# Retention and a mixture of experts on one core: the query's decay applied on the way out of PSUM, another order of the second product's units, closing sums and low parts spread over more steps

## The chip, the cores and the metric

The kernel runs on one core of a Trainium2 chip. The metric is the device time of one execution in microseconds (us); less is better. Of the kernel before three runs are shown, and one execution was taken by the hardware profiler. PE is TensorE, DVE is VectorE, ACT is ScalarE, POOL is GpSimd, SP is SyncE, whose queue issues nearly all DMAs.

## The reference

```python
# retention: per head a decaying state, 4 batches, 8 heads, 768 steps, 64 wide
for t in range(S):
    state = gamma * state + einsum('bhd,bhe->bhde', k[:, :, t], v[:, :, t])
    y[:, :, t] = scale * einsum('bhd,bhde->bhe', q[:, :, t], state)
# x = y as [3072 tokens, 512]; then 4 experts, 512 -> 1024 -> 512
p = probs / (probs.sum(-1) + 1e-9)
out = sum over e of  p[:, e] * (maximum(x @ w1[e], 0) @ w2[e])
```

All inputs and outputs are fp32.

## The kernel before, in words

**Retention.** Each batch of 768 tokens is cut into 6 chunks of 128. For a chunk, `scores` multiplies k and q of all heads (16 small matmuls, L140) into two PSUM banks, DVE multiplies them with a mask (L143), `state` adds the chunk's k times v to the running state (L155, L157, L159), POOL scales that by the decay of a chunk (`decay`, L165), and `values` forms the output of the chunk in two halves: q times the state before (L182) and masked scores times v (L188), in two PSUM banks, each of which ACT then copies into `xraw` (L197). Two factors are put on by POOL beforehand: `scale_q` (L124) multiplies the chunk's q in place by a table `qs` (scale times a power of the head's decay), `scale_v` (L128) multiplies v by a table `ks`.

**Experts.** A fast scheme with seven products in place of eight is used for both products of each expert, so that x and the hidden activations appear as seven combinations each, numbered 1 to 7. Each operand is split into a high part (ACT, fp32r) and a low part (the rest), and each product is three matmuls (high high, high low, low high) of 128x384. A **round** n (64 of them, 16 for each batch) makes 256 hidden columns: 7 **steps**, one `p1` each (6 matmuls, L502), in the order `SEQ`. Seven combinations of x serve a batch: in the last round of a batch each step issues `x_hi` of the next batch (ACT, L236), and one step later `x_lo` (L240; POOL for steps 1 and 3, DVE for the five others), through the list `late`.

**Second product.** In batch 0 (rounds 0 to 15) `p2` (L537) computes it plainly while weights are prepared and stored to DRAM. From batch 1 on, hidden columns are made by `gated` (DVE L454, POOL subtractions L456), split by `op_hi` (ACT L442) and `op_lo` (L447: on POOL for combinations 5, 7, 6 and 4, named in `LO_POOL`, else on DVE), and consumed by `unit(q, k)`: for a pair q of rounds 14 units, 6 matmuls each (L563), in the order `UNITS`, a combination i and a half d (0, 1) per unit. Pair q's units are issued in the steps of the next two rounds, one behind each `p1`, so that a step of 6 + 6 matmuls takes about 2.08 us. Units use two PSUM banks in turn; `add` on DVE (L420) adds each unit's result to one of 14 running sums. So a unit's matmuls wait until DVE has added the unit two before.

**Closing.** With the last pair of a batch, `finish` (L573) combines the seven sums of each half into four outputs by additions in SBUF (L576), on POOL and DVE by the table in the code, and stores them (L582, SP queue). For batches 1 and 2 that happens in the first two rounds of the next batch, while x's low parts are also due; for batch 3 after the last round, in a tail of 14 units that have no `p1` beside them.

**Order.** All is issued in one hand-written order. `soon` holds pairs (steps to wait, action), and `pass_step` runs what is due at the start of a step. `att_steps` is a generator that issues the attention of the next batch in pieces between the steps of the present one; the main loop takes one piece every few steps. At the start of a chunk it issues `decay`, `scale_q` and `scale_v`; the first `scores` of a batch comes right behind them. Before round 0 the six chunks of batch 0 run by themselves, with the first weights and x's parts prepared on DVE, ACT and POOL (the start-up, up to about 46 us).

Of the kernel before, what the change touches and what calls it, by code (L numbers as in the profile page):

```python
# [14 lines left out]
C = 128  # L15
# [24 lines left out]

UNITS = tuple((i, d) for i in (1, 3, 5, 7, 6, 2, 4) for d in range(2))
A2_AT = {1: 0, 2: 2, 4: 3, 6: 4, 7: 5, 3: 6, 5: 7}
LO_POOL = (5, 7, 6, 4)


@with_exitstack
def retention_moe(ctx: ExitStack, tc: tile.TileContext, qk, kv, w1, w2, probs, probt, cmask, cqs, cks, cys, out, out_t):
# [29 lines left out]
    ps_a = ep(tc.tile_pool(name="ps_a", bufs=2, space=PS))  # L79

    mask = const.tile([128, C], F32, name="mask")
    qs = const.tile([128, NPAIR, C], F32, name="qs")
    ks = const.tile([128, H], F32, name="ks")
    ys = const.tile([128, NPAIR], F32, name="ys")

# [36 lines left out]
    def scale_q(ci, eng=nc.gpsimd):
        q = raw_qk[ci][:, 0]
        eng.tensor_tensor(out=q, in0=q, in1=qs, op=ALU.mult)  # L124

    def scale_v(ci):
        v = raw_kv[ci][:, 1]
# [42 lines left out]
    def values(ci, half):  # L170

        b, c = divmod(ci, NCHB)
        v = raw_kv[ci]
        sp = sprime[ci]
        if half == 0:
            pvs[ci] = [att_bank("ps_v"), att_bank("ps_v")]
        ps = pvs[ci]
        quad = [(r, k) for r in range(2) for k in range(2)]
        if c > 0:
            for r, k in quad:  # L180
                rows, p = slice(64 * r, 64 * r + 64), 2 * half + k
# [12 lines left out]
        if c == 0:  # L194
            xraw[b] = xr_p.tile([128, NPAIR, S], F32, tag="xr", name="xr")
        for r in range(2):
            nc.scalar.activation(out=xraw[b][:, 2 * r:2 * r + 2, c * C:(c + 1) * C], in_=ps[r][:, 0:2, :], func=ACTF.Copy)  # L197


    xcomb = {}  # L200
# [371 lines left out]

    def finish(b, i, d):  # L573
        p = {j: psum[b, j, d] for j in range(1, 8)}
        e1, e2 = (nc.gpsimd, nc.vector) if b < B - 1 else (nc.vector, nc.gpsimd)
        sums = lambda e, o, x: e.tensor_tensor(out=p[o], in0=p[o], in1=p[x], op=ALU.add)  # L576

        def store(j, f, h):

            rows = out_t[256 * f + 128 * d:256 * f + 128 * d + 128]  # L580
            to = rows[:, (b - 1) * S + HB * h:(b - 1) * S + HB * h + HB]
            soon.append((2, lambda: nc.sync.dma_start(out=to, in_=p[j])))  # L582

        if i == 1:
            sums(e1, 2, 1)
        elif i == 5:
            sums(e1, 3, 5)
        elif i == 6:
            sums(e2, 6, 1)
            sums(e2, 7, 6)  # L590
            sums(e2, 4, 7)
            sums(e1, 3, 6)
            store(3, 0, 1)
            sums(e1, 5, 7)
            store(5, 1, 1)
        elif i == 2:
            store(2, 0, 0)
        elif i == 4:
            store(4, 1, 0)


    def att_steps(b):
        ci0 = b * NCHB
        load_qk(ci0 + 1)
        for ci in range(ci0, ci0 + NCHB):
            old = ci > ci0
            decay(ci)
# [24 lines left out]
    with tc.manual_schedule():  # L632
# [1 line left out]
        nc.vector.memset(warm, 0.0)  # L634
        load_qk(0)
        load_kv(0, eng=nc.scalar)
        nc.sync.dma_start(out=qs, in_=cqs)
        nc.scalar.dma_start(out=ks, in_=cks)
        nc.scalar.dma_start(out=mask, in_=cmask)
        load_qk(1, v_p, "w2h")  # L640
        load_kv(1)
        nc.scalar.dma_start(out=ys, in_=cys)
# [57 lines left out]
        values(ci, 1)  # L700

        steps = iter(())
        late = []
        for n in range(NRND * B):
            g, r = divmod(n, NRND)
            if r == 0 and g + 1 < B:
# [9 lines left out]
            for k, i in enumerate(SEQ if n else FIRST):  # L716
# [52 lines left out]
def _layout(q, k, v, moe_domain_probs, moe_w1, moe_w2):  # L769
# [26 lines left out]
    cqs = scale * gp[:, :, None] ** (t + 1 - C)[None, None, :]  # L796
# [22 lines left out]
```

## Time and profile before

| | us |
|---|---|
| runs, median (lowest to highest) | 1109.12 (1108.71 to 1111.15), 3 runs |
| the profiled execution | 1108.82 |
| its span | 1106.7 |
| PE busy in the span | 1069.9 (97%) |
| DVE, ACT, POOL busy | 716.0 (65%), 391.9 (35%), 707.5 (64%) |

The span runs from the first to the last instruction of the profiled execution; 2.1 us of that execution lie outside it. Busy times are averages over very unlike stretches: the start-up, batch 0, three batches with units, and the tail. The page's slices show PE at 9 tenths or more in most of the 40 slices, and less in the first, in two in the middle and in the last. The granted clock is 2.4 GHz (1.0 in the profile's rows) or half of it (0.5); a row's figure is a mean over its stretch.

### The profile page before, as it was taken

The numbers are of one execution on the slowest core, as the hardware profiler recorded it, in microseconds if no ns is written. First come the engines' busy times: TensorE is split into PE (matmuls) and PEld (weight loads), VectorE is DVE, ScalarE is ACT, GpSimd is POOL, SyncE is SP. The second block draws the span as 40 slices with busy tenths as digits, with TensorE's granted clock in tenths as the row PEclk, the third lists the DMA queues.
The fourth block names the chain that finished last, engine by engine and source line by source line (L and its number), as shares of the span: only waits on it lengthen the run. The fifth ranks groups of instructions, "written<-read, shape, count | busy, mean of one in ns | idle before, by whom it ended". The sixth has DMA issues, their size and how long they took to land.

```text
span 1106.7 us, 18610 instructions
## 1 busy us (share of the span) xinstructions
PE 1069.9 (97%) x6696; PEld 996.6 (90%) x6696; DVE 716.0 (65%) x1174; ACT 391.9 (35%) x785; POOL 707.5 (64%) x661
## 2 busy tenths in 40 slices
PE   7889999999999999999998999999999899999996
PEld 5678888888889999999998999999999899999995
DVE  5767566666676466666685455676668746667665
ACT  2434444444434422322341433223234343333230
POOL 5668676766637754754677666557468855555555
PEclk9899999999999999999998999999999999999998
DMA  8499989898899777877886887887788888887874
GB/s 319 143 307 306 305 304 354 290 321 296 266 340 321 248 259 261 263 241 259 255 252 212 283 272 218 277 269 221 236 254 252 275 265 255 264 261 251 266 221 152
DMA packets 154603, 293.70 MB, mean 265 GB/s; under 512 B 12688, under 2 KB 77328, under 8 KB 154512
## 3 DMA queue, kind: packets, MB, share of 16 engines
q1 hardware_dynamic: 153936, 291.92, 80.9%
q8 instruction: 53, 0.87, 0.3%
q10 hardware_dynamic: 576, 0.60, 0.2%
q14 instruction: 38, 0.31, 0.1%
HBM read 223.22 MB, written 69.26 MB: 264 GB/s over the span
## 4 chain that ended last, share of the span: by engine, by line
PE 87%; DVE 5%; POOL 4%; issue 3%; DMA 1%; ACT 0%; SPq 0%; POOLq 0%; DVEq 0%; ACTq 0%
PE ps_u L563 30%; PE ps_x L502 23%; PE ps_z L502 11%; PE ps_o L537 10%; PE ps_y L502 6%; PE ps_v L188 2%; PE ps_s L140 2%; DVE xl L240 1%; PE ps_v L182 1%; DVE sum L576 1%; PE ps_y L155 1%; POOL sum L576 1%; POOL qk L124 1%; POOL ol L447 1%; DVE sum L420 1%
## 5 line engine op out<-in xcount | busy, mean ns | idle before, releaser
L563 PE MATMUL ps_u<-oh,v 128*128 128x384 f32 x1344 | 397.9, 338 | 13.2 <-DVE sum L420 13.1
L456 POOL TENSOR_TENSOR b<-b 128x384 f32<-128x384 f32 x192 | 206.7, 1077 | 146.4 <-DVE b L454 118.2
L447 POOL TENSOR_TENSOR ol<-b,oh 128x384 fp32r<-128x384 f32 x192 | 208.2, 1096 | 101.6 <-ACT oh L442 51.9
L563 PEld LDWEIGHTS ps_u<-oh,v 128*128 128x128 f32 x1344 | 249.7, 189 | 16.6 <-DVE sum L420 16.6
L420 DVE TENSOR_TENSOR sum<-ps_u,sum 128x384 f32<-128x384 f32 x294 | 162.0, 552 | 146.4 <-PE ps_u L563 146.3
L442 ACT ACTIVATE oh<-b 128x384 fp32r<-128x384 f32 x336 | 163.0, 520 | 196.6 <-POOL b L456 106.9
L502 PE MATMUL ps_x<-xh,v 128*128 128x384 f32 x768 | 229.5, 340 | 0.3 <-ACT u L414 0.3
L563 PE MATMUL ps_u<-ol,v 128*128 128x384 f32 x672 | 226.1, 337 | 0.0
L414 ACT ACTIVATE u<-ps_x 128x384 f32<-128x384 f32 x128 | 62.7, 490 | 248.3 <-PE ps_x L502 248.1
L502 PEld LDWEIGHTS ps_x<-xh,v 128*128 128x128 f32 x768 | 142.4, 189 | 4.2 <-issue 2.3
L447 DVE TENSOR_TENSOR ol<-b,oh 128x384 fp32r<-128x384 f32 x144 | 127.3, 884 | 12.9 <-ACT oh L442 12.9
L502 PE MATMUL ps_x<-xl,v 128*128 128x384 f32 x384 | 129.1, 336 | 0.0
L563 PEld LDWEIGHTS ps_u<-ol,v 128*128 128x128 f32 x672 | 127.4, 190 | 0.0
L502 PE MATMUL ps_z<-xh,v 128*128 128x384 f32 x384 | 114.7, 339 | 0.4 <-DVE xl L240 0.3
L545 DVE SCALAR_TENSOR_TENSOR acc<-ps_o,pm,acc 128x512 f32<-128x512 f32 x90 | 67.0, 745 | 59.7 <-PE ps_o L537 59.7
L537 PE MATMUL ps_o<-w2h,hl 128*128 128x512 f32 x192 | 75.8, 395 | 0.0
L537 PE MATMUL ps_o<-w2l,hh 128*128 128x512 f32 x192 | 75.8, 395 | 0.0
L537 PE MATMUL ps_o<-w2h,hh 128*128 128x512 f32 x192 | 75.2, 392 | 0.0
L502 PEld LDWEIGHTS ps_z<-xh,v 128*128 128x128 f32 x384 | 70.8, 188 | 2.8 <-issue 1.0
L502 PEld LDWEIGHTS ps_x<-xl,v 128*128 128x128 f32 x384 | 72.5, 189 | 0.1
L502 PE MATMUL ps_z<-xl,v 128*128 128x384 f32 x192 | 64.2, 334 | 0.0
L420 DVE TENSOR_TENSOR ps_y<-ps_y,u 128x384 f32<-128x384 f32 x64 | 36.1, 565 | 40.6 <-PE ps_y L502 40.6
(108 smaller groups left out, 1680.7 us busy)
## 6 DMA issues: line engine op xcount, KB each, us to landing
v<-k SPq DMA_DIRECT2D x336, 256.0 KB, 3.7
v<-k SPq DMA_DIRECT2D x168, 512.0 KB, 4.4
k<-w1h SPq DMA_DIRECT2D x16, 896.0 KB, 6.3
k<-w1l SPq DMA_DIRECT2D x16, 896.0 KB, 8.5
qk<-in_qk SPq DMA_DIRECT2D x24, 512.0 KB, 5.9
kv<-in_kv SPq DMA_DIRECT2D x23, 512.0 KB, 6.4
w1r<-in_w SPq DMA_DIRECT2D x16, 512.0 KB, 7.9
w2r<-in_w SPq DMA_DIRECT2D x16, 512.0 KB, 4.2
```

The source lines that it names most:

```text
L140: nc.tensor.matmul(ps[r][:, p, :], lhsT=a[rows, 1, p, :], rhs=a[rows, 0, p, :], start=True, stop=True)
L188: nc.tensor.matmul(ps[r][64 * k:64 * k + 64, half, :], lhsT=v[:, 1, h, :], rhs=sp[:, h, :], start=(c == 0), stop=True, skip_group_check=True,)
L414: nc.scalar.activation(out=t, in_=ps, func=ACTF.Copy)
L420: nc.vector.tensor_tensor(out=o, in0=ps, in1=u, op=ALU.add)
L442: nc.scalar.activation(out=hi, in_=t, func=ACTF.Copy)
L447: eng.tensor_tensor(out=lo, in0=t, in1=hi.bitcast(F32), op=ALU.subtract)
L456: sub = lambda o, a, b: nc.gpsimd.tensor_tensor(out=o, in0=a, in1=b, op=ALU.subtract)
L502: nc.tensor.matmul(ps, lhsT=lhsT[:, cs], rhs=rhs[:, kt, :], start=(fresh and m == 0), stop=(m == 5), skip_group_check=True,)
L537: nc.tensor.matmul(ps, lhsT=a[:, ts], rhs=b[:, fs, :], start=(m == 0), stop=(m == 5))
L545: nc.vector.scalar_tensor_tensor(out=acc[nt], in0=ps, scalar=sc, in1=acc[nt], op0=ALU.mult, op1=ALU.add)
L563: nc.tensor.matmul(ps, lhsT=w[:, r, l, ds], rhs=o, start=(m == 0), stop=(m == 5))
L576: sums = lambda e, o, x: e.tensor_tensor(out=p[o], in0=p[o], in1=p[x], op=ALU.add)
```

## The change

1. `scale_q` goes, with its 24 POOL instructions. The table `qs` is laid out by bank and loaded on ACT's queue behind the mask, not second on SP's. Where `values` left PSUM by two ACT copies for each chunk (48 in all), DVE now multiplies each bank by `qs[:, r]` into `xraw`.
2. `UNITS` has the combinations in the order 1, 3, 6, 7, 5, 4, 2 in place of 1, 3, 5, 7, 6, 2, 4.
3. `finish`: per half, POOL does 2+=1, 6+=1, 7+=6, 4+=7, 7+=5 and DVE 3+=6, 3+=5, in all batches, each through `soon` with a wait of 0 to 2 steps. Before, POOL did 2+=1, 3+=5, 3+=6, 5+=7 and DVE 6+=1, 7+=6, 4+=7 at once (engines the other way round in batch 3). 4+=7 is now added to sum 4 ahead of the last unit of that sum. The four stores follow with waits of 0 to 2.
4. `x_lo` is issued up to 5 steps after its `x_hi` (`XLATE`) for batches 2 and 3, through `soon`.

The core of the diff:

```diff
-UNITS = tuple((i, d) for i in (1, 3, 5, 7, 6, 2, 4) for d in range(2))
+UNITS = tuple((i, d) for i in (1, 3, 6, 7, 5, 4, 2) for d in range(2))
+XLATE = (1, 2, 2, 3, 4, 4, 5)
-    qs = const.tile([128, NPAIR, C], F32, name="qs")
+    qs = const.tile([128, 2, 2, C], F32, name="qs")
-    def scale_q(ci, eng=nc.gpsimd):
-        q = raw_qk[ci][:, 0]
-        eng.tensor_tensor(out=q, in0=q, in1=qs, op=ALU.mult)
         for r in range(2):
-            nc.scalar.activation(out=xraw[b][:, 2 * r:2 * r + 2, c * C:(c + 1) * C], in_=ps[r][:, 0:2, :], func=ACTF.Copy)
+            o = xraw[b][:, 2 * r:2 * r + 2, c * C:(c + 1) * C]
+            nc.vector.tensor_tensor(out=o, in0=ps[r][:, 0:2, :], in1=qs[:, r], op=ALU.mult)
...
-        e1, e2 = (nc.gpsimd, nc.vector) if b < B - 1 else (nc.vector, nc.gpsimd)
-        sums = lambda e, o, x: e.tensor_tensor(out=p[o], in0=p[o], in1=p[x], op=ALU.add)
+        e1, e2 = nc.gpsimd, nc.vector
+        def sums(wait, e, o, x):
+            soon.append((wait, lambda: e.tensor_tensor(out=p[o], in0=p[o], in1=p[x], op=ALU.add)))
-        def store(j, f, h):
+        def store(wait, j, f, h):
...
         if i == 1:
-            sums(e1, 2, 1)
-        elif i == 5:
-            sums(e1, 3, 5)
-        elif i == 6:
-            sums(e2, 6, 1)
-            sums(e2, 7, 6)
-            sums(e2, 4, 7)
-            sums(e1, 3, 6)
-            store(3, 0, 1)
-            sums(e1, 5, 7)
-            store(5, 1, 1)
+            sums(0, e1, 2, 1)
+        elif i == 6:
+            sums(0, e1, 6, 1)
+            sums(2, e2, 3, 6)
+        elif i == 7:
+            sums(0, e1, 7, 6)
+            sums(1, e1, 4, 7)
+        elif i == 5:
+            sums(0, e1, 7, 5)
+            sums(0, e2, 3, 5)
+            store(2, 7, 1, 1)
+            store(2, 3, 0, 1)
+        elif i == 4:
+            store(1, 4, 1, 0)
         elif i == 2:
-            store(2, 0, 0)
-        elif i == 4:
-            store(4, 1, 0)
+            store(0, 2, 0, 0)
...
                     x_hi(g + 1, i)
-                    late.append(lambda b=g + 1, i=i, e=nc.gpsimd if k in XPOOL else nc.vector: x_lo(b, i, eng=e))
+                    e = nc.gpsimd if k in XPOOL else nc.vector
+                    soon.append((XLATE[k] - 1 if g else 0, lambda b=g + 1, i=i, e=e: x_lo(b, i, eng=e)))
```

What the change moves, at three places. Numbers behind a name tell one buffer from another; a line number above 124 is up to two less in the changed kernel, and L576 became L578.

POOL, first steps of batch 2 (round 32). The names: `sum` are the running sums, `ol` low parts of combinations, `b` their subtractions, `qk` and `kv` the first chunk of batch 3. Before:

```order
L456 TENSOR_TENSOR b_6206<-b_6206,b_6174 128x384
L576 TENSOR_TENSOR sum_3875<-sum_3875,sum_3582 128x384
L447 TENSOR_TENSOR ol_6304<-b_6174,oh_6303 128x384
L576 TENSOR_TENSOR sum_3902<-sum_3902,sum_3609 128x384
L447 TENSOR_TENSOR ol_6331<-b_6234,oh_6330 128x384
L447 TENSOR_TENSOR ol_6334<-b_6206,oh_6333 128x384
L456 TENSOR_TENSOR b_6259<-b_6259,b_6206 128x384
L124 TENSOR_TENSOR qk_5323<-qk_5323,qs_112 128x512
L128 TENSOR_TENSOR kv_5325<-kv_5325,ks_113 128x512
```

and now:

```order
L456 TENSOR_TENSOR b_6188<-b_6188,b_6156 128x384
L447 TENSOR_TENSOR ol_6283<-b_6156,oh_6282 128x384
L578 TENSOR_TENSOR sum_3915<-sum_3915,sum_3568 128x384
L447 TENSOR_TENSOR ol_6310<-b_6215,oh_6309 128x384
L447 TENSOR_TENSOR ol_6313<-b_6188,oh_6312 128x384
L578 TENSOR_TENSOR sum_3947<-sum_3947,sum_3595 128x384
L456 TENSOR_TENSOR b_6240<-b_6240,b_6188 128x384
L127 TENSOR_TENSOR kv_5307<-kv_5307,ks_113 128x512
```

The multiplication of `qk` is gone, and each sum stands one low part later.

DVE, round 33, from the units 6 and 7 on. `sum<-ps_u` is a unit's addition, `sum<-sum` a closing one. Before:

```order
L420 TENSOR_TENSOR sum_3813<-ps_u_6524,sum_3813 128x384
L576 TENSOR_TENSOR sum_3813<-sum_3813,sum_3582 128x384
L576 TENSOR_TENSOR sum_3761<-sum_3761,sum_3813 128x384
L576 TENSOR_TENSOR sum_3929<-sum_3929,sum_3761 128x384
L447 TENSOR_TENSOR ol_6511<-b_6460,oh_6510 128x384
L420 TENSOR_TENSOR sum_3851<-ps_u_6556,sum_3851 128x384
L576 TENSOR_TENSOR sum_3851<-sum_3851,sum_3609 128x384
L576 TENSOR_TENSOR sum_3784<-sum_3784,sum_3851 128x384
L576 TENSOR_TENSOR sum_3962<-sum_3962,sum_3784 128x384
L420 TENSOR_TENSOR ps_y_6572<-ps_y_6572,u_6484 128x384
```

and now:

```order
L420 TENSOR_TENSOR sum_3747<-ps_u_6445,sum_3747 128x384
L578 TENSOR_TENSOR sum_3636<-sum_3636,sum_3687 128x384
L420 TENSOR_TENSOR sum_3770<-ps_u_6469,sum_3770 128x384
L156 COPY yst0_115<-ps_y_6477 128x256
L578 TENSOR_TENSOR sum_3658<-sum_3658,sum_3725 128x384
L420 TENSOR_TENSOR sum_3799<-ps_u_6510,sum_3799 128x384
L447 TENSOR_TENSOR ol_6495<-b_6441,oh_6494 128x384
L578 TENSOR_TENSOR sum_3636<-sum_3636,sum_3799 128x384
L420 TENSOR_TENSOR sum_3837<-ps_u_6540,sum_3837 128x384
L578 TENSOR_TENSOR sum_3658<-sum_3658,sum_3837 128x384
L420 TENSOR_TENSOR ps_y_6553<-ps_y_6553,u_6467 128x384
```

Two runs of three closing sums have become four single ones with a unit's addition between them; of these, the first two read sums 6 (3687, 3725), to which POOL has added 1.

POOL, the tail, to the end of the program. Before:

```order
L447 TENSOR_TENSOR ol_12238<-b_12169,oh_12237 128x384
L576 TENSOR_TENSOR sum_9989<-sum_9989,sum_9780 128x384
L576 TENSOR_TENSOR sum_9937<-sum_9937,sum_9989 128x384
L576 TENSOR_TENSOR sum_10095<-sum_10095,sum_9937 128x384
L576 TENSOR_TENSOR sum_10017<-sum_10017,sum_9808 128x384
L576 TENSOR_TENSOR sum_9960<-sum_9960,sum_10017 128x384
L576 TENSOR_TENSOR sum_10115<-sum_10115,sum_9960 128x384
```

and now, from the low parts of 5, 7 and 6 on:

```order
L447 TENSOR_TENSOR ol_12169<-b_12078,oh_12168 128x384
L578 TENSOR_TENSOR sum_10071<-sum_10071,sum_9758 128x384
L447 TENSOR_TENSOR ol_12185<-b_12126,oh_12184 128x384
L447 TENSOR_TENSOR ol_12188<-b_12104,oh_12187 128x384
L578 TENSOR_TENSOR sum_10091<-sum_10091,sum_9785 128x384
L456 TENSOR_TENSOR b_12145<-b_12145,b_12104 128x384
L447 TENSOR_TENSOR ol_12214<-b_12145,oh_12213 128x384
L578 TENSOR_TENSOR sum_9866<-sum_9866,sum_9758 128x384
...
L578 TENSOR_TENSOR sum_9936<-sum_9936,sum_9993 128x384
```

POOL's six sums at the end have become ten, of which two stand between and behind the low parts; rows left out are six more sums.

## Rows read from the trace of the kernel before

**Rows 1.** Window: PE, PEld, DVE, ACT, POOL busy; granted clock, DMA share, GB/s.

```profile
345.00:570.00 225.00, 224.97 (x1481) 215.18 (x1480) 140.40 (x246) 78.59 (x172) 142.60 (x134) 1.00 0.80 259
```

**Rows 2.** Waits of PE over the whole span: us in total, times, longest.

```profile
PE ps_u L563 <- DVE sum L420: 13.1, 9, 2.6
```

**Rows 3.** Timeline of PE: start, duration, instruction, [idle before, releaser]; scores.

```profile
61.62 1.99 PE L140 MATMUL ps_s<-qk 64*128 64x128 f32 x16 [2.41 <-POOL qk L124]
584.66 2.08 PE L140 MATMUL ps_s<-qk 64*128 64x128 f32 x16 [4.09 <-POOL qk L124]
```

**Rows 4.** Timeline of PE: units at the two batch ends.

```profile
575.08 0.45 PE L563 MATMUL ps_u<-oh,v 128*128 128x384 f32 x1 [1.21 <-DVE sum L420]
609.93 0.44 PE L563 MATMUL ps_u<-oh,v 128*128 128x384 f32 x1 [1.79 <-DVE sum L420]
845.40 0.44 PE L563 MATMUL ps_u<-oh,v 128*128 128x384 f32 x1 [1.22 <-DVE sum L420]
867.10 0.45 PE L563 MATMUL ps_u<-oh,v 128*128 128x384 f32 x1 [0.60 <-DVE sum L420]
872.07 0.45 PE L563 MATMUL ps_u<-oh,v 128*128 128x384 f32 x1 [2.59 <-DVE sum L420]
```

**Rows 5.** Windows around the four drops of the granted clock (PEclk, third from the end).

```profile
61.00:66.00 5.00, 4.38 (x25) 4.07 (x26) 2.81 (x4) 1.44 (x2) 3.00 (x4) 0.66 1.07 380
583.00:592.00 9.00, 7.34 (x36) 7.12 (x37) 3.44 (x7) 1.46 (x3) 3.06 (x4) 0.62 0.43 147
611.00:615.00 4.00, 4.00 (x16) 4.00 (x15) 3.90 (x9) 0.57 (x2) 4.00 (x4) 0.57 0.85 257
1095.00:1104.00 9.00, 5.81 (x18) 4.99 (x18) 3.55 (x7) 0.00 (x0) 4.45 (x4) 0.62 0.37 132
```

**Rows 6.** Groups by line: busy, mean ns of one | idle before, releasers.

```profile
L124 POOL TENSOR_TENSOR qk<-qk,qs 128x512 f32<-128x512 f32 x24 | 32.3, 1345 | 6.6 <-DMA qs<-in_cqs 6.6
L197 ACT ACTIVATE xr<-ps_v 128x256 f32<-128x256 f32 x48 | 15.8, 380 | 43.7 <-PE ps_v L188 43.7
L159 DVE TENSOR_TENSOR yst<-ps_y,yst 128x256 f32<-128x256 f32 x16 | 6.8, 422 | 12.1 <-PE ps_y L155 11.9
L576 DVE TENSOR_TENSOR sum<-sum 128x384 f32<-128x384 f32 x20 | 18.0, 899 | 4.8 <-POOL sum L576 4.3
```

**Rows 7.** Timeline of DVE at the end of batch 1.

```profile
604.92 3.35 DVE L576 TENSOR_TENSOR sum<-sum 128x384 f32<-128x384 f32 x3
```

**Rows 8.** Timeline of POOL: the multiplication of q that PE waits for at 584.66.

```profile
583.34 1.27 POOL L124 TENSOR_TENSOR qk<-qk,qs 128x512 f32<-128x512 f32 x1
```

**Rows 9.** Timeline of POOL and then of PE in a steady pair of rounds of batch 3.

```profile
908.80 2.31 POOL L447 TENSOR_TENSOR ol<-b,oh 128x384 fp32r<-128x384 f32 x2 [1.06 <-PE ps_u L563]
914.50 0.33 PE L563 MATMUL ps_u<-ol,v 128*128 128x384 f32 x1
```

**Rows 10.** Timeline of the tail: a unit on PE, POOL, DVE's last addition.

```profile
1078.12 0.33 PE L563 MATMUL ps_u<-oh,v 128*128 128x384 f32 x1
1081.37 3.90 POOL L447 TENSOR_TENSOR ol<-b,oh 128x384 fp32r<-128x384 f32 x3
1091.87 7.74 POOL L576 TENSOR_TENSOR sum<-sum 128x384 f32<-128x384 f32 x6 [3.98 <-DVE sum L420]
1103.34 0.56 DVE L420 TENSOR_TENSOR sum<-ps_u,sum 128x384 f32<-128x384 f32 x1 [1.18 <-PE ps_u L563]
```

**Rows 11.** Timeline of DVE in the start-up, and POOL's q of the fourth chunk.

```profile
15.09 1.01 DVE L265 TENSOR_TENSOR s<-w1r 128x256 f32<-128x256 f32 x1 [0.96 <-DMA w1r<-in_w]
16.14 1.38 DVE L266 TENSOR_TENSOR s<-s,w1r 128x256 f32<-128x256 f32 x1
17.55 0.42 DVE L267 TENSOR_TENSOR s<-w1r,s 128x256 f32<-128x256 f32 x1
31.02 0.42 DVE L159 TENSOR_TENSOR yst<-ps_y,yst 128x256 f32<-128x256 f32 x1 [0.81 <-PE ps_y L155]
15.78 1.46 POOL L124 TENSOR_TENSOR qk<-qk,qs 128x512 f32<-128x512 f32 x1
```

More of the change, by code (lines that the diff above doesn't have):

```diff
@@ L574, in finish @@
         p = {j: psum[b, j, d] for j in range(1, 8)}
-        e1, e2 = (nc.gpsimd, nc.vector) if b < B - 1 else (nc.vector, nc.gpsimd)
-        sums = lambda e, o, x: e.tensor_tensor(out=p[o], in0=p[o], in1=p[x], op=ALU.add)
-        def store(j, f, h):
+        e1, e2 = nc.gpsimd, nc.vector
+        def sums(wait, e, o, x):
+            soon.append((wait, lambda: e.tensor_tensor(out=p[o], in0=p[o], in1=p[x], op=ALU.add)))
+        def store(wait, j, f, h):
             rows = out_t[256 * f + 128 * d:256 * f + 128 * d + 128]
             to = rows[:, (b - 1) * S + HB * h:(b - 1) * S + HB * h + HB]
-            soon.append((2, lambda: nc.sync.dma_start(out=to, in_=p[j])))
+            soon.append((wait, lambda: nc.sync.dma_start(out=to, in_=p[j])))
         if i == 1:
-            sums(e1, 2, 1)
-        elif i == 5:
-            sums(e1, 3, 5)
-        elif i == 6:
-            sums(e2, 6, 1)
-            sums(e2, 7, 6)
-            sums(e2, 4, 7)
-            sums(e1, 3, 6)
-            store(3, 0, 1)
-            sums(e1, 5, 7)
-            store(5, 1, 1)
+            sums(0, e1, 2, 1)
[5 more added lines that the diff above has]
+            sums(1, e1, 4, 7)
+        elif i == 5:
+            sums(0, e1, 7, 5)
[4 more added lines that the diff above has]
+            store(1, 4, 1, 0)
         elif i == 2:
-            store(2, 0, 0)
-        elif i == 4:
-            store(4, 1, 0)
+            store(0, 2, 0, 0)
     def att_steps(b):
@@ L607, in att_steps @@
             decay(ci)
-            scale_q(ci)
             scale_v(ci)
@@ L636, in retention_moe @@
         load_kv(0, eng=nc.scalar)
-        nc.sync.dma_start(out=qs, in_=cqs)
         nc.scalar.dma_start(out=ks, in_=cks)
         nc.scalar.dma_start(out=mask, in_=cmask)
+        nc.scalar.dma_start(out=qs, in_=cqs)
         load_qk(1, v_p, "w2h")
@@ L658, in retention_moe @@
             nc.tensor.matmul(wps[:, 0:w], lhsT=warm[:, 0:128], rhs=warm[:, 0:w], start=True, stop=True)
-        scale_q(0)
         for ci in range(NCHB):
@@ L662, in retention_moe @@
             scale_v(ci)
-            if ci + 1 < NCHB:
-                scale_q(ci + 1)
             scores(ci)
@@ L702, in retention_moe @@
         steps = iter(())
-        late = []
         for n in range(NRND * B):
@@ L741, in retention_moe @@
                         p2(n - 1, tiles.pop(0))
-                if late:
-                    late.pop()()
                 if r == NRND - 1 and g + 1 < B:
                     x_hi(g + 1, i)
-                    late.append(lambda b=g + 1, i=i, e=nc.gpsimd if k in XPOOL else nc.vector: x_lo(b, i, eng=e))
+                    e = nc.gpsimd if k in XPOOL else nc.vector
+                    soon.append((XLATE[k] - 1 if g else 0, lambda b=g + 1, i=i, e=e: x_lo(b, i, eng=e)))
                 if n < NRND:
@@ L795, in _layout @@
     gp = gamma.reshape(NPAIR, 2).T.repeat(D, axis=0)
-    cqs = scale * gp[:, :, None] ** (t + 1 - C)[None, None, :]
+    gq = gamma.reshape(2, 2, 2).transpose(1, 2, 0).repeat(D, axis=0)
+    cqs = scale * gq[..., None] ** (t + 1 - C)
     cks = gamma[None, :] ** (C - 1 - t)[:, None]
```

## The prediction, made before the changed kernel ran

> **What bounds the kernel now.** I read the busy times first, then the windows, then PE's waits, then the timeline around each wait. In a long middle stretch PE is busy for 224.97 of 225 us at full clock, with DVE at 140.4 and POOL at 142.6 [rows 1]; the same holds of the rest of batches 0 to 3. There nothing is to be won without fewer matmuls, and the change has as many as before. What is to be won lies in a few stalls. PE waits nine times for a unit's addition on DVE, 13.1 us in total [rows 2], and at the first scores of batches 1 and 3 for POOL's multiplication of q, 2.41 and 4.09 us [rows 3]. The reader is to see a second price beside each stall: behind these four places the granted clock falls from 2.4 to 1.2 GHz for some 3.4 or 6.8 us, so that the window's mean is 0.57 to 0.66 [rows 5]. What a drop costs is (1 less the mean) times the window.
>
> The sum is made against the profiled execution, 1108.8 us; that is 0.3 below the median of the three runs. A difference under 0.2% (2.2 us) can't be told from none.
>
> **A, the first scores of batch 1.** q is no longer touched by POOL, whose instruction is gone, and its transfer has long landed; the 2.41 us go. The drop behind costs 0.34 x 5 = 1.7 us [rows 5] and goes with its cause: -4.1.
>
> **B, the first scores of batch 3.** POOL works off closing sums and low parts and reaches q at 583.34 [rows 8]. The 4.09 us go, and 0.38 x 9 = 3.4 us of clock, of which I leave out 0.3 because PE still waited in part of it: -7.2. The scores next need only their two PSUM banks, free since a chunk earlier.
>
> **C, the two batch ends.** Five waits [rows 4]: 1.21 + 1.79 + 1.22 + 0.60 + 2.59 = 7.4 us, and 0.43 x 4 = 1.7 us of clock behind the second. Their cause on DVE is a run of three closing sums of 3.35 us, in front of additions that PE needs [rows 7], and the five low parts of x. Now DVE has four single sums in place of six, and the low parts come over more steps. So -9.1. I give 1 us back at each end: the addition of unit 4 now waits for POOL's 4+=7, at the end of a POOL chain (6+=1, 7+=6, 4+=7 for both halves), and everything behind it on DVE waits too. Net -7.1.
>
> **D, the tail.** Of the 13.1 us, 13.1 - 7.4 = 5.7 lie here, with 3.4 us of clock [rows 5], of which some 2.4 fell on work: 8.1 us. Most of that comes back. A unit takes 1.04 us here; the last one of the steps starts at 1078.12 [rows 10], so without stalls the tail's unit number 5, which is now the first of combination 6, would need its low part at 1079.2 + 4 x 1.04 + 0.7 = 1084.0. POOL ended the three low parts at 1081.37 + 3.90 = 1085.3 [rows 10], and now has one sum of 7.74 / 6 = 1.3 us among them: a stall of 2.5 us. After the low part of 4, POOL has six sums to the second 4+=7, from about 1089.5 to 1097.2 (1095.5 at 1.0 each); the addition, the last unit and its addition end at about 1100. Before, the last addition ended at 1103.9 [rows 10]. With a clock drop behind the stall I take -3; the bounds are -6 (a POOL without contention) and +2 (a drop as long as before and POOL at 1.3 us).
>
> **E, the start-up.** DVE is what sets the end here, from the landing of the first weights at 15.09. It gets two multiplications for each of chunks 2 to 6, out of PSUM. The nearest row is the update of the state, the same shape, one operand in PSUM: 0.42 us [rows 6]; ten of them are 4.2 us. Against that: DVE stood idle 0.81 us at 31.02; and its two weight sums beside POOL's q of chunk 4 took 1.01 and 1.38 us, the third, of the same shape, 0.42 [rows 11]. If that q was the reason, (1.01 + 1.38 - 2 x 0.42) = 1.55 us come back. I take 4.2 - 0.8 - 1.6 = +1.8; the bounds are -1 (the other POOL multiplications of q slowed DVE as well) and +4.2 (none did, and no idle time absorbs anything). The Trainium skill, SBUF — State Buffer, section "Who interferes with whom", has DVE and GpSimd share one pair of ports as an exclusive lock, taken by a DVE operation with two SBUF inputs against a GpSimd operation that reads SBUF. By that rule all 1.55 us come back and the new multiplications, with one operand in PSUM, are not held themselves, so E is +1.8; by the 0.42 rows alone it would be +3.4.
>
> **What is hidden.** Later on DVE has 12 more multiplications for each batch, 5 us in 290, in stretches where it is busy 62% of the time [rows 1]; POOL loses 24 x 1.345 us and ACT 48 x 0.38 [rows 6], neither on the path there. If DVE's cover were gone, each would cost 0.42 us. On SP one store at a batch end now waits for POOL's 7+=5 with weight fetches behind it; these are issued four steps (8.3 us) ahead, so a delay of a few us costs nothing. The Trainium skill, Advanced Engine Details and Errata, section "The Read-Write Bubble", says that ScalarE is nearer to PSUM and VectorE to SBUF, which speaks against taking PSUM out with DVE. Rows 6 show 0.38 us on ACT and 0.42 on DVE, and by that rule the sum is no other, since DVE does the multiplication in the same pass.
>
> **Sum:** -4.1 - 7.2 - 7.1 - 3 + 1.8 = -19.6; 1108.8 - 19.6 = **1089.2 us**.
>
> **Rivals.**
>
> *The batch ends stay bound (0.20).* POOL's sums go from 22 to 30 and the chain to 4+=7 is longer than DVE's order allows. For: a DVE sum in SBUF takes 0.90 us on average [rows 6] against 0.56 for the last addition with POOL idle, so both engines are slow there. Against: the low parts of x no longer fall together. Price: at each of the two ends a wait like the longest, 2.59, and a clock drop of 1.7, 8.6 in place of the 2 given back: 1095.8. The Trainium skill, Perfetto Trace Analysis, section "Optimizing Scalar/DVE Operations", warns that moving work between GpSimd and DVE may not help, since they share a port. If that decides, the batch ends come out as in this rival.
>
> *Start-up and tail at their bad ends (0.08).* E +4.2 and D +2: 1089.2 + 2.4 + 5 = 1096.6.
>
> *The stalls at the scores find a successor (0.06).* PE goes on 4 and 7 us earlier and meets the next late thing (a low part of x, a unit's addition), so that A and B change name and not size: 1089.2 + 11.3 = 1100.5. For: at 575 DVE was behind just before B. Against: 240 us without a stall follow A.
>
> *Slower: unit 6 outruns POOL (0.05).* Unit 6 comes four steps (8.3 us) earlier, before units 7 and 5. In a steady pair POOL ends the low part of 6 at 908.80 + 2.31 = 911.1, and the place at which it will be needed is 914.5 [rows 9]: 3.4 us in hand. If POOL came later than that by t us in each of 24 pairs, the cost is 24 x t: the gain is used up at t = 0.8, so from a delay of 4.2 us on the kernel is slower; at 4.5 it would be 1089.2 + 26 = 1115. For: the margin was 11.7 us before the units moved. Against: POOL has less to do in every chunk, by 1.3 us.
>
> **How the numbers follow.** My forecast has 0.61 and by the bounds of D and E its own range is 1083 to 1095. The first rival stretches the top to 1096, the second to 1097; the third reaches 1100.5. From 1082 to 1100 is left out the last rival, some of the third and a little at the bottom: under 0.2. Faster by over 0.2% are all cases but the last, with something taken off for what I didn't see: 0.92; within 0.2%: 0.03; slower: 0.05.
>
> **What would show it.** A and B right: no wait of scores for POOL, and granted clock 1.0 from 61 to 66 and from 583 to 592. C right: no wait, or one under 1 us, of units for DVE behind each batch end, with single closing sums on DVE. D right: one wait of PE for POOL's low part near the fifth unit of the tail, and a last addition 3 us nearer to the last `p1`. E right: the first round's weights and x parts end 1 to 3 us later than before on DVE, and the sums at 15 us take 0.42. Wrong would be many short waits of units for POOL's low parts, or DVE's addition of unit 4 waiting for POOL by more than 2 us.

## The result, and the profile after

| | before | changed |
|---|---|---|
| median of 4 runs (lowest to highest) | 1108.91 (1105.1 to 1111.15) | 1096.81 (1095.32 to 1097.05) |
| profiled execution, its span | 1108.82, 1106.7 | 1096.67, 1094.7 |

The ratio is 0.9892, 95% interval 0.9863 to 0.992: faster, by 12.1 us. The forecast was 1089.2. The time lies in the stated range (1082 to 1100), but 7.6 us above the forecast and outside the range of the forecast's own case (1083 to 1095); it is near the first rival's 1095.8.

Engine totals on the page of the changed kernel; then, in the view of waits, what PE waited for (us in total, times, longest), to be held against [rows 2]:

```profile
PE 1062.9 (97%) x6696; PEld 990.3 (90%) x6696; DVE 718.6 (66%) x1214; ACT 380.2 (35%) x737; POOL 685.0 (63%) x645
```

```profile
PE ps_u L563 <- DVE sum L420: 6.4, 5, 2.8
...
PE ps_x L502 <- ACT u L414: 3.4, 4, 1.5
...
PE ps_u L563 <- POOL ol L447: 1.1, 1, 1.1
PE ps_z L502 <- DMA v<-k: 1.0, 1, 1.0
```

The scores' wait for q is gone. Units wait for additions 6.4 us instead of 13.1. A new wait for a transfer (`v<-k`, weights fetched back from DRAM) has come, and one for a low part from POOL.

The timeline of PE in the changed kernel shows where:

```profile
38.86 0.69 PE L502 MATMUL ps_x<-xh,w1h 128*128 128x384 f32 x1
...
64.84 0.44 PE L502 MATMUL ps_x<-xh,w1h 128*128 128x384 f32 x1 [0.92 <-ACT u L414]
69.17 0.49 PE L537 MATMUL ps_o<-w2h,hh 128*128 128x512 f32 x1 [0.58 <-DVE acc L543]
87.25 0.49 PE L537 MATMUL ps_o<-w2h,hh 128*128 128x512 f32 x1 [0.53 <-DVE acc L545]
319.17 0.41 PE L502 MATMUL ps_z<-xh,v 128*128 128x384 f32 x1 [1.04 <-DMA v<-k]
605.46 0.44 PE L563 MATMUL ps_u<-oh,v 128*128 128x384 f32 x1 [1.11 <-DVE sum L420]
860.21 0.44 PE L563 MATMUL ps_u<-oh,v 128*128 128x384 f32 x1 [0.66 <-DVE sum L420]
865.43 0.59 PE L563 MATMUL ps_u<-oh,v 128*128 128x384 f32 x1 [2.84 <-DVE sum L420]
1076.09 0.44 PE L563 MATMUL ps_u<-ol,v 128*128 128x384 f32 x1 [1.13 <-POOL ol L447]
1082.49 0.44 PE L563 MATMUL ps_u<-oh,v 128*128 128x384 f32 x1 [1.60 <-DVE sum L420]
```

And its windows (columns as in [rows 5], PEclk third from the end):

```profile
61.00:66.00 5.00, 4.08 (x25) 3.34 (x22) 1.56 (x2) 1.44 (x2) 1.58 (x3) 1.00 0.98 338
583.00:592.00 9.00, 9.00 (x65) 8.68 (x64) 8.13 (x15) 3.38 (x8) 8.04 (x7) 1.00 0.85 282
865.00:870.00 5.00, 4.57 (x17) 4.57 (x18) 3.40 (x5) 1.81 (x4) 4.22 (x4) 0.66 1.01 289
```

The drops at 61 and 583 are gone, and a new one has come behind the longest wait, at 865.

To put the difference in its place, both traces were read at the start of the same `p1`. The table gives the changed kernel's start less that of before, and what lies between two places.

| first `p1` of | before | changed | difference | in between |
|---|---|---|---|---|
| round 0 | 37.75 | 38.86 | +1.1 | start-up (E) +1.1 |
| round 3 | 91.39 | 91.19 | -0.2 | first scores of batch 1 (A) -1.3 |
| round 19 | 361.08 | 361.47 | +0.4 | wait for a transfer at 319: +0.6 |
| round 35 | 631.40 | 621.20 | -10.2 | scores of batch 3 (B) -7.0; first batch end -3.6 |
| round 51 | 889.88 | 880.63 | -9.25 | second batch end +0.95 |
| end of span | 1106.7 | 1094.7 | -12.0 | tail (D) -2.7 |

Between rounds 19 and 35, B is what the two steps around the scores at 584 us gained; the rest belongs to the batch end.

### The profile page after: what moved, and what is told of

Its sections match the earlier page's. It is cut to its first block, busy times and chain, and to the rows that moved or that the text cites. A ratio compares the mean times of both kernels' runs of the same rounds, so it can differ in the third digit from the quotient of the medians.

```text
span 1094.7 us, 18567 instructions
## 1 busy us (share of the span) xinstructions
PE 1062.9 (97%) x6696; PEld 990.3 (90%) x6696; DVE 718.6 (66%) x1214; ACT 380.2 (35%) x737; POOL 685.0 (63%) x645
## 4 chain that ended last, share of the span: by engine, by line
PE 84%; DVE 5%; POOL 4%; issue 3%; DMA 2%; ACT 1%; SPq 0%; ACTq 0%; POOLq 0%; DVEq 0%
PE ps_u L563 30%; PE ps_x L502 22%; PE ps_z L502 11%; PE ps_o L537 10%; PE ps_y L502 6%; PE ps_v L187 2%; PE ps_s L139 2%; POOL sum L578 1%; PE ps_v L181 1%; DVE xl L240 1%; POOL b L456 1%; DMA w2r<-in_w 1%; PE ps_y L154 1%; DMA w1r<-in_w 1%; DMA ks<-in_cks 1%
## 5 line engine op out<-in xcount | busy, mean ns | idle before, releaser
L447 DVE TENSOR_TENSOR ol<-b,oh 128x384 fp32r<-128x384 f32 x144 | 122.0, 848 | 12.6 <-ACT oh L442 12.6
```

The lines of the kernel that those rows point to most:

```text
L447: eng.tensor_tensor(out=lo, in0=t, in1=hi.bitcast(F32), op=ALU.subtract)
```

## The experiments

Waits are from PE's timeline of the one profiled execution of each kernel; ratios are to runs of before on the same chip (medians 1109.2 to 1109.9). The tail is counted from the start of the last `p1` to the end of the span: 29.6 us before, 26.9 in the changed kernel.

**The parts by themselves.** Before, with the decay moved alone:

```diff
...
-            nc.scalar.activation(out=xraw[b][...], in_=ps[r][:, 0:2, :], func=ACTF.Copy)
+            nc.vector.tensor_tensor(out=o, in0=ps[r][:, 0:2, :], in1=qs[:, r], op=ALU.mult)
...
-            scale_q(ci)
...
```

> The kernel before with the decay alone moved: q no longer scaled on POOL, DVE multiplies by qs where the values leave PSUM; old order of units, old closing sums, old low parts of x. My theory (of the 12.1 us that the change won, about 7 are the stall at the first scores of batch 3, and the start-up and the first scores of batch 1 nearly cancel): start-up +1.1, from there to round 4 -1.3, scores of batch 3 -7.0, tail unchanged: about -7, 1101 to 1103 us, and PE's waits at 575, 610, 845, 867 and 872 within 0.5 us of what they were. Rival (DVE's extra 5 us for each batch are what made the second batch end no better): the waits of units for DVE at the two batch ends grow by over 2 us together, and the gain is 5 us or less.

Measured: 1103.16, ratio 0.9935 [0.9912, 0.9958], just above the range that was expected. B is there in full (-7.0), and the waits at the batch ends stand as in [rows 4], to 0.02 us. So DVE's extra multiplications don't hold the batch ends; what is new there comes from the sums and the low parts. In the profiled execution 2.1 us were lost to transfers between rounds 16 and 19, and 1.6 to a clock drop at the second batch end, behind a wait that had none before (last section).

Before, with the new order of units and the new closing sums alone. Against the changed kernel that is the decay put back (ACT copies, POOL multiplies q) and x's low parts not spread:

```diff
-            nc.vector.tensor_tensor(out=o, in0=ps[r][:, 0:2, :], in1=qs[:, r], op=ALU.mult)
+            nc.scalar.activation(out=xraw[b][...], in_=ps[r][:, 0:2, :], func=ACTF.Copy)
...
+            scale_q(ci)
...
-                    soon.append((XLATE[k] - 1 if g else 0, lambda b=g + 1, i=i, e=e: x_lo(b, i, eng=e)))
+                    late.append(lambda b=g + 1, i=i, e=nc.gpsimd if k in XPOOL else nc.vector: x_lo(b, i, eng=e))
```

> The kernel before with the new order of units and the new closing sums alone; q still scaled on POOL. My theory (the tail gains 2.8 us, the first batch end 3.6 less 1.3, the second loses 1): the scores of batches 1 and 3 still wait about 2.4 and 4 us for POOL, the tail is 2.8 us shorter, the stalls behind units 4 stay, about -4 in all: 1104 to 1106 us. Rival (the closing sums won nothing by themselves, and the gain at the first batch end comes from the missing q or from the low parts): tail -2.8 only, batch ends 0 or worse: 1106 to 1109 us.

Measured: 1102.12, 0.993 [0.9914, 0.9946], 2 us less than either theory expected. The scores wait again, 2.41 and 3.48 us. The two waits of 1.22 at the starts of the batch ends (573.67 and 839.79) are still there; behind them no unit waits at the first end, and at the second one waits 2.82 us. By the starts of the rounds, the first end (rounds 33 to 35) gains 3.65 us, the second 0.6, and the tail is 2.7 us shorter than before, as in the changed kernel, so D belongs to this part. Of the 9.0 us that the profiled execution gained, some 1.5 lie in round 1, where the clock did not drop (last section).

The changed kernel without the spread alone:

```diff
-                    soon.append((XLATE[k] - 1 if g else 0, lambda b=g + 1, i=i, e=e: x_lo(b, i, eng=e)))
+                    soon.append((0, lambda b=g + 1, i=i, e=e: x_lo(b, i, eng=e)))
```

> The changed kernel with every low part of x issued one step after its high part, as before the change. My theory (the spread took away the two waits of 1.2 us at 575 and 845, and nothing else): both come back, +2.5 us, 1098.5 to 1100.5 us, and a clock drop behind them would add up to 1.7 each. Rival (DVE is not late there any more because the units' order and the sums changed): within 0.5 us of the changed kernel. Second rival (the spread costs more later than it wins): 1 to 3 us faster, with shorter waits at 605 and 865.

Measured: 1098.79, 0.9904 [0.9886, 0.9922]. Four waits of 0.55, 1.37, 0.56 and 1.34 come back at the starts of the two ends (575, 579, 836, 840), the one at 605 goes, and the one at 869 is 2.44. By the starts of the rounds the two ends are 1.0 and 0.6 us worse without the spread. The medians differ by 2.0 us, but the two intervals overlap.

**The batch ends.** The second one in the changed kernel, on POOL's timeline:

```profile
848.02 4.10 POOL L456 TENSOR_TENSOR b<-b 128x384 f32<-128x384 f32 x3
852.09 1.33 POOL L578 TENSOR_TENSOR sum<-sum 128x384 f32<-128x384 f32 x1
853.38 1.33 POOL L447 TENSOR_TENSOR ol<-b,oh 128x384 fp32r<-128x384 f32 x1
854.66 1.99 POOL L578 TENSOR_TENSOR sum<-sum 128x384 f32<-128x384 f32 x2
856.60 1.99 POOL L447 TENSOR_TENSOR ol<-b,oh 128x384 fp32r<-128x384 f32 x2
858.54 1.98 POOL L578 TENSOR_TENSOR sum<-sum 128x384 f32<-128x384 f32 x2
860.46 1.03 POOL L456 TENSOR_TENSOR b<-b 128x384 f32<-128x384 f32 x1
```

No row has a gap before it: POOL is busy throughout. ACT's timeline, and then DVE's, of the same place:

```profile
861.53 1.35 ACT L442 ACTIVATE oh<-b 128x384 fp32r<-128x384 f32 x3 [8.46 <-POOL b L456]
```

```profile
859.60 0.56 DVE L420 TENSOR_TENSOR sum<-ps_u,sum 128x384 f32<-128x384 f32 x1 [2.27 <-POOL sum L578]
862.50 1.34 DVE L447 TENSOR_TENSOR ol<-b,oh 128x384 fp32r<-128x384 f32 x1 [2.34 <-ACT oh L442]
```

Two chains run from POOL's sums to PE. In the first, the second addition of unit 4 on DVE waits 2.27 us for 4+=7. In the second, `b` of combination 4 (860.46) stands on POOL behind 4+=7 and 7+=5; ACT's `oh` of 4, first in ACT's order, waits 8.46 us for it, with the `oh` of 1 behind; DVE's low part of 1 waits 2.34 us for that, with unit additions behind; PE waits 2.84 us at 865.43. The theory is that these two chains are the whole shortfall of C. Both fall if 4+=7 and 7+=5 are issued behind unit 4:

```diff
-            sums(1, e1, 4, 7)
...
-            sums(0, e1, 7, 5)
-            store(2, 7, 1, 1)
...
-            store(1, 4, 1, 0)
...
+            sums(0, e1, 4, 7)
+            sums(0, e1, 7, 5)
+            store(2, 4, 1, 0)
+            store(2, 7, 1, 1)
```

> The changed kernel with 4+=7 and 7+=5 issued behind unit 4's additions (both stores 2 steps later). In the profile of the changed kernel POOL is busy without a gap from 846.8 to 863.4 behind the second batch end; the subtraction for combination 4 stands behind two closing sums, ACT's two high parts and DVE's low part behind it, and DVE's addition of unit 4 waits 2.27 us for 4+=7. My theory (POOL's queue at the batch ends is the bound, closing sums stand ahead of work that PE needs): the stalls at 605 (1.1 us) and 860 and 865 (0.7 and 2.8, with a clock drop of 1.7 behind) go, tail within 1 us: -4.5 to -6.3, 1090.5 to 1092.5 us. Rival A (only the addition of unit 4 waiting is the cause): the same gain here, but none in the run with 7+=5 on DVE. Rival B (DVE is the bound there): the stalls stay within 0.7 us.

Measured: 1091.01, 0.9832 [0.9812, 0.9851]. POOL's `b` of 4, the waits of PE and the windows at both ends:

```profile
857.15 1.02 POOL L456 TENSOR_TENSOR b<-b 128x384 f32<-128x384 f32 x1
```

```profile
PE ps_u L563 <- DVE sum L420: 2.0, 3, 1.6
```

```profile
602.00:608.00 6.00, 6.00 (x37) 6.00 (x36) 3.44 (x6) 0.98 (x2) 5.92 (x7) 1.00 0.81 276
860.00:870.00 10.00, 9.82 (x56) 9.26 (x55) 4.50 (x9) 4.87 (x11) 9.76 (x10) 1.00 0.77 256
```

`b` of 4 ends 2.9 us earlier, counted from the start of round 48; of the waits at the two ends 0.18 us is left (the rest of the 2.0 lies in the tail), and the clock stays at 1.0. Read as in the table above, the ends give -5.0 and -4.0, against -3.6 and +0.95: together -9.0, where the working had 9.1 to win. So the theory holds: same sums on the same engines, only later in POOL's order. The run takes both chains away at once; it doesn't part what each costs alone.

With 7+=5 alone moved, to DVE and a step later:

```diff
-            sums(0, e1, 7, 5)
+            sums(1, e2, 7, 5)
...
-            store(2, 7, 1, 1)
+            store(3, 7, 1, 1)
```

> The changed kernel with 7+=5 on DVE one step later, in place of POOL. My theory (POOL's queue): one sum less ahead of the subtraction for combination 4, so that it starts about 1 us earlier and the stall at 865 shrinks by about 1 us, to 1.5 to 2.2; a tail with two POOL sums less, 0 to -1: -1 to -2.5 in all, 1094.3 to 1095.8. Rival A (only the addition of unit 4 that waits for 4+=7): that wait stays at 2.3 and the stall at 865 at 2.8, no change. Rival B (DVE is the bound): two more sums of 0.8 to 1.4 us on DVE make the stall longer, by 1 us or more.

Measured: 1095.51, 0.9872 [0.9853, 0.9891]. At the second end one wait of 2.12 us (861.40) stands in place of two; at the first, DVE is late instead, 0.86 and 0.51 us (603.31, 607.23). By the starts of the rounds the second end is 1.5 us better than in the changed kernel, the first 0.9 worse, and the tail 1.3 better. The chain to 4+=7 has only moved: in this run's timeline it is 7+=5 on DVE that waits for it, with the units' additions behind.

```profile
857.18 2.63 DVE L578 TENSOR_TENSOR sum<-sum 128x384 f32<-128x384 f32 x2 [2.38 <-POOL sum L578]
```

**What follows the scores of batch 1.** ACT's timeline in the changed kernel:

```profile
63.35 1.06 ACT L286 ACTIVATE w2h<-w2r 128x1024 fp32r<-128x1024 f32 x1 [4.82 <-DMA w2r<-in_w]
64.31 0.47 ACT L414 ACTIVATE u<-ps_x 128x384 f32<-128x384 f32 x1
```

`u`, which PE's wait at 64.84 is for, stands on ACT behind `w2h`, and that behind a transfer of w2. The same wait stood in the trace of before, where PE was still held by the scores:

```profile
62.09 1.06 ACT L286 ACTIVATE w2h<-w2r 128x1024 fp32r<-128x1024 f32 x1 [4.53 <-DMA w2r<-in_w]
```

These preparations put a step later in rounds 1 and 2:

```diff
-            hi2(n, wt2, "w2")
+            if n > 2:
+                hi2(n, wt2, "w2")
...
-            lo2(n, wt2, nc.vector)
+            if n > 2:
+                lo2(n, wt2, nc.vector)
+            else:
+                hi2(n, wt2, "w2")
...
+            if n <= 2:
+                lo2(n, wt2, nc.vector)
```

> The changed kernel with the high and low part of the second product's weights one step later in rounds 1 and 2 (step 2 and 3 in place of 1 and 2). My theory (at the first scores of batch 1 the gain of 4.1 was taken back because ACT waits 4.8 us for the transfer of these weights at 63.35, with the copies of p1's banks behind it, and DVE's low part behind that): the waits of PE at 64.84 (ACT u, 1.1), 69.17 (0.75) and 87.25 (0.7) go or halve: -1 to -2.4, 1094.4 to 1096. Rival (POOL or DVE are simply late by their own work in rounds 1 to 3): no change, or the same loss at other places.

Measured: 1095.61, 0.9874 [0.9859, 0.9889]. The three waits of 64.84, 69.17 and 87.25 are gone; from round 0 to round 3 the gain on before is 4.2 us (the forecast's A, 4.1) in place of 1.3. By round 19 a wait for the low part of w1 (0.92 at 91.96) and one of 1.51 for the transfer at 318.32 have taken most of the difference back: 0.5 us is left of it at round 19. The other 0.6 us by which its span is shorter than the changed kernel's came later: at the second batch end the wait is the same (2.85 at 865.16), but in this execution no clock drop followed it. So rounds 0 to 3 show what stood behind A, and the total does not show what the later w2 is worth.

**The transfers at 319.** The first four weight fetches of round 16 issued ahead of two stores:

```diff
-                fetch_w1(t + 4)
+                first_w = 7 * NRND
+                if t in (first_w - 6, first_w - 5):
+                    fetch_w1(2 * t - first_w + 12)
+                    fetch_w1(2 * t - first_w + 13)
+                elif not first_w - 4 <= t < first_w:
+                    fetch_w1(t + 4)
```

> The changed kernel with the first four weight fetches of round 16 issued in steps 1 and 2 of round 15, ahead of two stores of weights, in place of steps 3 to 6. In the traces so far PE comes to round 16's second step between 315 and 317.5 us and waits 0.7 to 2.2 us there for these weights, which land at 318.4 to 319.5 whatever the start-up has won or lost. My theory (what is won before round 16 is taken back by this transfer): the wait at 319 goes and nothing takes its place: -0.8 to -1.2, about 1095.7 us. Rival (the queue is full there in any order, DMA share 0.96 to 0.99): the wait moves to a later weight and the time is within 0.4 us of the changed kernel.

Measured: 1096.86, 0.988 [0.9863, 0.9898]: no gain. The wait at 319 goes, and others come (0.78 at 321.62, 0.65 at 348.09). In the windows from 305 to 345 us the DMA engines are busy for 0.99 of the time before and 0.96 in the changed kernel. The rival was right: moving these fetches moved the wait.

Nor is the loss between rounds 16 and 19 the price of an earlier gain. Four runs whose code is the same up to there (the changed kernel, the late sums, 7+=5 on DVE, the tail) come to round 16 between 0.2 and 0.4 us ahead of before and lose 0.6, 1.75, 1.55 and 0.9 us in these three rounds; the decay alone, 0.2 behind, loses 2.1.

**The start-up.** Batch 0's values copied by ACT, without the decay:

```diff
-            nc.vector.tensor_tensor(out=o, in0=ps[r][:, 0:2, :], in1=qs[:, r], op=ALU.mult)
+            if b == 0:
+                nc.scalar.activation(out=o, in_=ps[r][:, 0:2, :], func=ACTF.Copy)
+            else:
+                nc.vector.tensor_tensor(out=o, in0=ps[r][:, 0:2, :], in1=qs[:, r], op=ALU.mult)
```

> The changed kernel with the values of batch 0 copied by ACT, as before the change, without the multiplication by the query's decay (so batch 0's outputs lack that factor); measures what the twelve multiplications on DVE cost in the start-up. My theory (DVE sets the end of the start-up; the multiplications cost more than the 1.1 us seen, because POOL's missing work gave some back): round 0 begins at 35.5 to 37 us in place of 38.9, and the total is lower by no more than 0.6 us, since the transfer at 319 takes the rest back. Rival (the start-up is slower for another cause, the later landing of qs or masks): round 0 begins at 38 or later.

Measured: 1095.4, 0.987 [0.9853, 0.9886]. Round 0 begins at 36.77, against 38.86 in the changed kernel and 37.75 before. So DVE's multiplications cost 2.1 us, and the rest of the change, above all POOL's missing work, gave 1.0 back. Each figure comes from single executions: in the ten traces with the changed kernel's start-up round 0 begins between 38.0 and 39.3, so none of them is sure to better than 1 us. The second half of the theory missed: the transfer at 319 did not take the gain back. PE's wait came 2.8 us earlier and was no longer (0.93 at 316.41), and the profiled execution's span was 2.3 us shorter than the changed kernel's, the median 1.4, where 0.6 at most was expected.

**The tail.** Two of the last batch's sums later, for earlier low parts:

```diff
-            sums(0, e1, 2, 1)
+            sums(5 if last else 0, e1, 2, 1)
-            sums(2, e2, 3, 6)
+            sums(4 if last else 2, e2, 3, 6)
```

> The changed kernel; in the last batch alone 2+=1 is issued 5 steps later on POOL and 3+=6 two steps later on DVE. In the profile of the changed kernel PE waits 1.1 us in the tail for POOL's low part of 6, behind 2+=1, and 1.6 us for DVE, whose additions stand behind 3+=6 that waits for POOL; 1080 to 1088 runs at a mean clock of 0.79. My theory (both are a matter of order alone): the two waits go and with them the clock drop of 1.7: the last p1 to the end shrinks by 3 to 4.4 us, 1092.4 to 1094. Rival (POOL's ten sums set the end in any order): the waits move to the additions of unit 4, less than 1.5 us in all.

Measured: 1097.79, 0.9892 [0.9872, 0.9911]: a miss. The wait for the low part (1.13) is gone, and waits of 1.20 and 1.22 for DVE's additions stand in its place (1083.87, 1086.42); the tail is 26.9 us as in the changed kernel. The eight output stores show why. On SP's timeline and in the view of SP's waits, first of the changed kernel, then of this run:

```profile
1087.68 4.02 SPq L584 DMA_DIRECT2D out<-sum  x8
SPq L584 <- POOL sum L578: 7.4, 1, 7.4
```

```profile
1087.76 4.02 SPq L585 DMA_DIRECT2D out<-sum  x8
SPq L585 <- POOL sum L579: 8.3, 1, 8.3
```

The first store waits for POOL's first 7+=5, which ends at 1087.7 in both; the others stand behind it in SP's order, and the span ends 3.0 us after the last is issued. DVE's last addition ends 1.0 us earlier than in the changed kernel (1089.37 against 1090.37), and that wins nothing. So the rival was right: POOL's sums, and the stores behind them, set the end of the tail.

**Together.** The later sums, the later w2 and this tail, with 7+=5 of the last batch on DVE:

```diff
...
+            sums(0, e1, 4, 7)
+            sums(1 if last else 0, e2 if last else e1, 7, 5)
...
```

> The changed kernel with late sums, weights of the second product a step later in rounds 1 and 2, the tail's order, and 7+=5 of the last batch on DVE. If the parts add up (-5.4 for the batch ends, -1.3 measured for the weights, -4 for the tail): about 1086 us, 1084.5 to 1088. If POOL's work in all is the bound at the batch ends and in the tail, half of that: 1091.

Measured: 1089.14, 0.9819 [0.9796, 0.9843], tail 25.5: 1.1 us above the range for parts that add up. The tail gave 1.4 of the 4 us it was given. Then also the early fetches, and the tail's sums on DVE one at a time between the units' additions:

```diff
-            sums(2, e2, 3, 6)
+            sums(3 if last else 2, e2, 3, 6)
...
-            sums(0, e2, 3, 5)
+            sums(1 if last else 0, e2, 3, 5)
...
```

> The run with all parts (late sums, weights later in rounds 1 and 2, tail's order) plus the early fetch of round 16's weights and, in the last batch, DVE's four closing sums one at a time between the units' additions. Against 1089.1: -1.3 for the transfer (what the start-up won comes through as well), -1 to -3 for the two waits of the tail (0.6 and 1.2 us) and the clock drop behind them: 1085 to 1087 us. If POOL's eight sums set the tail's end in any order, 1087 to 1088.

Measured: 1087.0 (1086.93 to 1088.12), 0.9797 [0.9782, 0.9812], tail 24.7: on the border between the theory and its rival, which it doesn't part. In its view of waits (its L569 is the units' line):

```profile
PE ps_u L569 <- DVE sum L426: 0.2, 1, 0.2
...
PE ps_u L569 <- POOL ol L453: 0.2, 1, 0.2
```

Of the units' waits for additions and low parts 0.4 us is left. This is the fastest version of the study, 9.8 us under the changed kernel by medians.

## Why the prediction was wrong in size

Forecast and measured, in us of span: A -4.1, -1.3; B -7.2, -7.0; C -7.1, -2.7; D -3, -2.7; E +1.8, +1.1; the transfer at 319, not foreseen, +0.6. Sums -19.6 and -12.0.

**C failed, at "I give 1 us back at each end".** The removal was sized well: 9.1 on paper, 9.0 when nothing new stands in its way (the late sums). What came back was 6.4 us, not 2: 1.4 at the first end and 5.0 at the second. The forecast named one chain, DVE's addition behind POOL's 4+=7, and priced it at 1 us; it waited 2.27, the sign that the text had set for being wrong. It did not see the second chain, POOL's sums ahead of `b` of 4, through ACT and DVE to PE. It could have been read before the run: the order of POOL showed the sums among the low parts, and ACT and DVE took their instructions in the order of the program. Behind the long wait came a clock drop of 0.34 x 5 = 1.7 us. The first rival was right in mechanism: POOL's longer chain of sums holds the batch ends. That its time fits (1095.8, measured 1096.8) is luck in part. It left C at 0.5 us of gain, and C gave 2.7; what A fell short by (2.8) and the transfer at 319 made up for that. The Trainium skill, Perfetto Trace Analysis, section "Optimizing Scalar/DVE Operations", warned that a move between GpSimd and DVE may not pay because of the shared port. Here the port was not what decided: the closing sums were slow on both engines (1175 and 961 ns on average in the groups by line of the changed kernel, below; the shortest took 994 and 550), but with the same sums on the same engines in a later order the stalls went, so the order did.

```profile
L578 POOL TENSOR_TENSOR sum<-sum 128x384 f32<-128x384 f32 x30 | 34.9, 1175 | 1.8 <-DVE sum L420 1.6
L578 DVE TENSOR_TENSOR sum<-sum 128x384 f32<-128x384 f32 x12 | 11.5, 961 | 1.4 <-POOL sum L578 1.2
L197 DVE TENSOR_TENSOR xr<-ps_v,qs 128x256 f32<-128x256 f32 x48 | 18.0, 417 | 5.2 <-PE ps_v L187 4.5
```

**A was half the third rival.** The wait and the drop went, as forecast, and PE met the next late thing three times within 26 us, w2's preparation on ACT behind its transfer. "240 us without a stall follow A" was read from a trace in which PE came later; with w2 out of the way the term is -4.2. Nothing shows that the wait at 319 is of the same kind: the other runs lost between 0.5 and 2.1 us there (3.4 in one, with a clock drop), and those that came to round 16 earliest did not lose the most. Why the one trace of before has next to none of it stays open; fetching earlier did not win it back.

**B was right.** Nothing stands behind it: PE is busy 9.00 of 9.00 us from 583 to 592. The slower rival, unit 6 outrunning POOL, did not come: PE's only wait for a low part of POOL is the 1.13 us in the tail.

**D was right in sum, in part by luck.** The wait for POOL's low part was 1.13, not 2.5; one of 1.60 for DVE's addition came with it, and the clock from 1080 to 1088 was 0.79 on average. DVE's last addition came 4.3 us nearer to the last `p1`, more than the 3 of the forecast. But the forecast ended its sum there and left out the stores, which behind POOL's sums took 1.6 us of that back: the span ends 4.4 us after that addition, where it was 2.8 before. Later sums on POOL alone made the tail 0.8 us shorter, and 7+=5 on DVE 1.3.

**E was right.** The ten multiplications took 0.417 us each (row above), 4.2 in all, but moved the start of round 0 by 2.1 only; the other 2.1 us presumably fell into idle time of DVE, for which the forecast had 0.8. The relief from POOL was 1.0 instead of 1.6, so that +1.1 came out for +1.8. The relief at the weight sums, on DVE's timeline:

```profile
15.05 0.84 DVE L265 TENSOR_TENSOR s<-w1r 128x256 f32<-128x256 f32 x1 [1.13 <-DMA w1r<-in_w]
15.93 0.42 DVE L266 TENSOR_TENSOR s<-s,w1r 128x256 f32<-128x256 f32 x1
```

They took 1.01 and 1.38 beside POOL's q [rows 11], and now 0.84 and 0.42: 1.13 of the 1.55 us. The 0.84 lies beside a POOL instruction that remains:

```profile
14.57 1.04 POOL L127 TENSOR_TENSOR kv<-kv,ks 128x512 f32<-128x512 f32 x1
```

The Trainium skill, SBUF — State Buffer, section "Who interferes with whom", makes this an exclusive lock between a DVE operation with two SBUF inputs and a GpSimd operation that reads SBUF. The rows agree: the sum of 1.38 before and that of 0.84 now both end 0.28 us after the POOL instruction beside them (17.52 behind 17.24, 15.89 behind 15.61), and the multiplications out of PSUM kept their 0.42.

## What to carry to other kernels

When work is moved into the order of an engine, follow from each instruction now behind it through every engine that takes its work in order (here POOL, ACT and DVE) to the one that bounds; the shortest chain is not the only one. When a stall is removed, look for what else arrives only just in time there, as the transfer of w2 did: it was hidden by the stall. And a closing sum that nobody waits for belongs behind the operands of the next units, even on the same engine. At the end of the program, follow the order of the stores as well.

## What was not expected of the hardware

The clock drop doesn't follow from the length of the wait alone. Before, the 2.41 us at 61.62 had one (0.66), the 2.59 us at 872.07 had none. With the decay alone the same 2.59 us (867.39) had one; with order and sums alone, 2.41 (61.02) and 2.82 us (869.95) had none. A wait of only 1.79 us had one before (609.93, [rows 4] and [rows 5]). The 2.84 us at 865.43 of the changed kernel had one (0.66), and the same 2.85 us with the later w2 had none. The windows behind 872.07, 867.39, 61.02 and 869.95, of before, of the decay alone, and of order and sums alone, and then the one behind 865.16 with the later w2:

```profile
872.00:877.00 5.00, 4.93 (x28) 4.93 (x29) 4.79 (x10) 1.84 (x4) 2.59 (x4) 1.00 0.94 300
```

```profile
867.00:872.00 5.00, 4.61 (x17) 4.61 (x18) 4.79 (x9) 1.46 (x3) 2.59 (x4) 0.66 0.79 243
```

```profile
60.00:66.00 6.00, 4.98 (x36) 4.51 (x37) 2.90 (x4) 1.63 (x3) 3.62 (x5) 1.00 1.04 370
869.00:875.00 6.00, 5.05 (x29) 5.05 (x30) 3.65 (x6) 3.31 (x8) 5.16 (x5) 1.00 1.03 319
```

```profile
865.00:870.00 5.00, 4.84 (x28) 4.84 (x29) 2.86 (x5) 3.09 (x8) 4.72 (x5) 1.00 0.96 271
```

So a term for a drop (1.7 us here) is one that may or may not be there. At 61 the drop was the larger part: round 1 took 24.06 us before, 22.59 with the wait and without the drop, 22.13 in the changed kernel with neither. What decides it was not settled.
